# Sparse attention and a multiplicative FFN in one kernel: the q and k transposes of six batches move from TensorE to the DMA engines

## The chip, the cores and the metric

The kernel runs on one core of one Trainium2 chip. The metric is the device time of one execution in microseconds (us). An execution that lies over 1.5% above the fastest one of the same kernel on the same chip counts as "slow"; only fast executions are compared. Each kernel was run beside the kernel before on the same chip.

The engines are TensorE (PE in the profile), VectorE (DVE), ScalarE (ACT), GpSimd (POOL) and SyncE (SP, which here only issues transfers). Where the first instruction in an engine's queue waits, those behind it wait too (shown below for DVE, for 6.06 us, and for ACT, for 3.80 us). The profile counts the transfers of all queues on the same 16 DMA engines.

## The reference, cut to what matters

```python
B, H, S, D = 8, 8, 576, 64              # q, k, v
# heads 0-3: 0 <= i - j < 32 ("local"); heads 4-7: j <= i and i % 32 == j % 32 ("strided")
attn = softmax(where(mask, q @ k.T / sqrt(D), -1e9)) @ v
x = attn.transpose(0, 2, 1, 3).reshape(B * S, H * D)        # 4608 x 512
h = (x @ w1) * (x @ w2)                                      # 4608 x 1024
return (h @ w3) @ w_out                                      # 4608 x 512
```

## The kernel before

The kernel folds `w3 @ w_out` into one matrix while it computes the attention of batch 0. It then runs nine FFN blocks ("stages"; stages 0 to 8) of 512 tokens each. Stage t hides the attention of batch t+1 between its own matmuls; stages 7 and 8 hide nothing. So stages 1 to 6 hide batches 2 to 7. The loads of batch t+2 are issued during stage t.

For the scores, q and k must have the head dimension on partitions. TensorE transposes them, and DVE and ACT copy the results out of PSUM:

```python
def ph_T(s):                                   # a pair of heads
    ps = psM.tile([P, 2, NM], FP16, tag="m")   # one bank in all
    for i, nm in enumerate("qk"):
        src = x16[(s.b, nm, s.hp // 2)]        # a buffer for each batch (pool of 2)
        for c in range(4):
            pe(nc.tensor.transpose(ps[:, i, c*P:(c+1)*P], src[:, c, h0:h0+2]..., id16))
    for i, (eng, t) in enumerate((("a", qT), ("a" if s.b < AHEAD else "v", kT))):
        copy(eng, t[...], ps[:, i]...)         # q by ACT, k by DVE
# ... ph_R: the same for the last 64 tokens of each head, all heads of a batch at once
```

The values v of the local heads need their rows shifted between token tiles. POOL casts the loaded v to fp16, and DVE then copies 32 partitions of the result:

```python
def load_vL(b):
    vt = v16L[b % 2]
    for hp in range(2):
        # ... st <- v by DMA
        for pr in (bass.ds(32, 32), bass.ds(64, 64)):
            nc.gpsimd.tensor_copy(out=vt[pr, hs, :, 0:D], in_=st[pr])
        nc.vector.tensor_copy(out=vt[0:32, hs, 1:LT, 0:D], in_=vt[96:P, hs, 0:LT-1, 0:D])
```

Everything that TensorE must do in a stage is put in one order: the units of the FFN, with the steps of the next batch's attention spread between them.

```python
def host(units, upto, lead=0):
    # ... after each FFN unit, as many attention steps as bring `pos` evenly to `upto`
for tch in range(1, NTILE):
    units = ab_halves(tch) + o_halves(tch)
    # ... load_qk(tch+2, 0), load_rest(tch+2), load_vL(tch+2)
    host(units[0:12], mid)
    # ... load_qk(tch+2, 1), load_vS(tch+2)
    host(units[12:], batch_end[tch + 1])
```

The softmax here doesn't subtract the row's maximum and nothing guards it: scores larger than these inputs give would overflow.

## Time and profile before

| | kernel before |
|---|---|
| time, median of 2 runs | 296.9 us |
| TensorE busy | 268.9 us of the profiled span of 299.8 us |
| start until stage 0 (fold, attention of batch 0) | 49.2 us |
| stages 1 to 6 | 29.1, 28.8, 27.8, 29.7, 27.8, 26.5 us |
| stage 7, which hides nothing | 21.0 us |
| last load packet | 185.3 us |

The first fence is from the page of the kernel before. Its rows are the busy time of the engines, the span in 40 slices with the busy share in tenths (PEclk is the clock that was granted to TensorE), the DMA packets, and the chain of work that ended last.

```profile
PE 268.9 (90%) x2401; PEld 141.6 (47%) x2401; DVE 174.6 (58%) x353; ACT 147.1 (49%) x269; POOL 102.1 (34%) x118
...
PE   2258898989889989989999899999999999999995
...
PEclk9996999999999999999999999999999999999999
DMA  7999999999869929994896796030012002003003
...
DMA packets 58653, 48.64 MB, mean 162 GB/s; under 512 B 29184, under 2 KB 49664, under 8 KB 58624
...
PE 67%; DVE 9%; DMA 9%; ACT 9%; issue 3%; SPq 1%; POOL 0%; ACTq 0%
```

TensorE is busy nearly all the time and makes up two thirds of the chain. The DMA row is at nine tenths from slice 2 to slice 10 (75 us), has gaps later, and is almost empty after slice 25: the loads run ahead of their use and are done with 115 us to go.

In every run with a listed span, the time is 1.7 us above the span. By that the profiled execution took about 301.5 us, which is 1.8% above the fastest run beside it: by the rule above it is a slow one.

The next fence is the view of windows for the kernel before, one line for the start and for some stages. The columns are the window, its length, the busy time of each engine with its number of instructions, the granted clock, the DMA share (1.00 and more is full) and what was moved.

```profile
core 0: us, PE busy (x) PEld busy (x) DVE busy (x) ACT busy (x) POOL busy (x), PEclk, DMA share, GB/s
0.00:49.20 49.20, 31.20 (x305) 18.26 (x306) 18.79 (x51) 21.80 (x39) 28.87 (x41) 0.93 1.04 289
...
84.70:113.70 29.00, 27.98 (x276) 14.72 (x273) 23.45 (x44) 14.92 (x29) 13.87 (x15) 1.00 0.85 201
113.70:142.50 28.80, 27.69 (x278) 14.93 (x275) 21.41 (x43) 15.14 (x30) 14.82 (x16) 1.00 0.92 212
```

A stage is TensorE's: 27.7 to 28.0 us of work in 28.8 to 29.0 us, at full clock.

The table of waits of the kernel before shows the small waits of TensorE at the stage starts. The columns are engine and line, what it waited for, the us in total, the number of times and the longest.

```profile
PE aps L312 <- ACT xT L291: 3.0, 5, 1.8
...
DVE v16L L182 <- POOL v16L L181: 1.9, 2, 1.6
```

### The profile page before, as it was taken

To read this page: it belongs to the slowest core of one execution; us is meant where nothing else is said; L and a number is where in the kernel's file an instruction comes from. 1 tells how busy PE (TensorE), PEld (TensorE's weight loads), DVE (VectorE), ACT (ScalarE), POOL (GpSimd) and SP (SyncE) were. 2 spreads that over 40 slices of the span, in tenths; PEclk is the share of its full clock that TensorE was granted. 3 is DMA by queue.
4 is the path that set the end of the run, shared out by engine and by line. 5 is a ranking of instruction groups with operands and counts; after the bars stand their busy time and mean duration, and the time that the engine had idled before them with its cause. 6 is when DMAs were issued, how large, how long until landed. Compare 5 with 4: busy or idle time off the path is not lost.

```text
span 299.8 us, 6132 instructions
## 1 busy us (share of the span) xinstructions
PE 268.9 (90%) x2401; PEld 141.6 (47%) x2401; DVE 174.6 (58%) x353; ACT 147.1 (49%) x269; POOL 102.1 (34%) x118
## 2 busy tenths in 40 slices
PE   2258898989889989989999899999999999999995
PEld 1025554435545545545555445555555555444442
DVE  2011775357888866886789659747765774340430
ACT  2025586557565545536645554564455445333332
POOL 5539744486626724653455345110000000000000
PEclk9996999999999999999999999999999999999999
DMA  7999999999869929994896796030012002003003
GB/s 228 349 160 352 288 348 258 216 273 209 249 200 243 242 79 270 246 178 159 240 236 140 253 193 164 27 115 2 2 57 87 0 2 105 35 2 116 24 2 140
DMA packets 58653, 48.64 MB, mean 162 GB/s; under 512 B 29184, under 2 KB 49664, under 8 KB 58624
## 3 DMA queue, kind: packets, MB, share of 16 engines
q1 hardware_dynamic: 53440, 38.81, 54.7%
q10 hardware_dynamic: 5184, 9.44, 8.7%
q8 instruction: 19, 0.31, 0.5%
q14 instruction: 10, 0.08, 0.1%
HBM read 38.80 MB, written 9.44 MB: 161 GB/s over the span
## 4 chain that ended last, share of the span: by engine, by line
PE 67%; DVE 9%; DMA 9%; ACT 9%; issue 3%; SPq 1%; POOL 0%; ACTq 0%
PE ops L335 19%; PE bps L321 18%; PE aps L312 16%; PE xps L268 4%; PE ps L214 4%; DMA st<-in_moe_w_dram 4%; ACT pte L253 3%; DVE ptm L255 3%; DMA st<-in_moe_w_out_dram 3%; DMA out_dram<-osb 3%; PE sps L248 2%; PE ps L284 2%; DVE abt L323 2%; ACT xT L291 2%; DVE kT L72 2%
## 5 line engine op out<-in xcount | busy, mean ns | idle before, releaser
L312 PE MATMUL aps<-xT,w1h 128*128 128x512 f16 x288 | 75.3, 379 | 3.2 <-ACT xT L291 3.0
L323 DVE TENSOR_TENSOR abt<-bps,asb 128x512 f16<-128x512 f32 x72 | 49.5, 687 | 47.2 <-PE bps L321 45.5
L321 PE MATMUL bps<-xT,w2h 128*128 128x512 f16 x288 | 74.0, 379 | 0.0
L315 ACT COPY asb<-aps 128x512 f32<-128x512 f32 x72 | 42.2, 586 | 64.6 <-PE aps L312 61.8
L335 PE MATMUL ops<-w,abt 128*128 128x512 f16 x288 | 71.7, 379 | 0.5 <-DVE abt L323 0.5
L74 POOL CAST t<-st 128x1024 f16<-128x1024 f32 (+1 forms) x48 | 47.4, 991 | 43.4 <-DMA st<-in_k_dram 29.1
L253 ACT ACTIVATE pte<-sps 128x576 f16<-128x576 f32 (+1 forms) x64 | 38.4, 650 | 7.3 <-PE sps L248 7.1
L276 DVE TENSOR_TENSOR xqs<-xps,rcp 96x384 f16<-96x384 f32 (+1 forms) x64 | 39.6, 619 | 2.0
L321 PEld LDWEIGHTS <-w2h 128*128 128x128 f16 x288 | 25.8, 97 | 31.6 <-issue 5.1
L70 ACT COPY qT<-ps 128x512 f16<-128x512 f16 (+1 forms) x48 | 22.9, 481 | 29.9 <-PE ps L214 23.8
L346 ACT COPY osb<-ops 128x512 f32<-128x512 f32 x36 | 21.1, 586 | 29.9 <-PE ops L335 28.6
L335 PEld LDWEIGHTS <-abt 128*128 128x128 f16 x288 | 24.7, 98 | 23.1 <-DVE abt L323 1.0
L312 PEld LDWEIGHTS <-w1h 128*128 128x128 f16 x288 | 25.1, 98 | 22.2
L181 POOL CAST v16L<-st 32x768 f16<-32x768 f32 (+1 forms) x32 | 27.1, 847 | 18.4 <-DMA st<-in_v_dram 12.6
L268 PEld LDWEIGHTS <-ptm 72*128 72x128 f16 (+1 forms) x448 | 21.4, 97 | 19.2 <-DVE ptm L255 6.4
L255 DVE TENSOR_TENSOR ptm<-pte,maskL 128x576 f16<-128x576 f16 x32 | 20.5, 646 | 11.7 <-ACT pte L253 11.2
L72 DVE COPY kT<-ps 128x512 f16<-128x512 f16 (+1 forms) x36 | 18.8, 535 | 10.1 <-ACT qT L70 10.0
L255 DVE TENSOR_TENSOR ptm<-pte,maskS 72x576 f16<-72x576 f16 x32 | 19.6, 620 | 8.5 <-ACT pte L253 7.9
L192 POOL CAST v16S<-st 72x1024 f16<-72x1024 f32 x16 | 16.9, 1055 | 20.1 <-PE xps L268 11.4
L335 PE MATMUL ops<-woh,w3T 128*128 128x512 f16 x64 | 19.8, 440 | 3.2 <-POOL woh L74 3.1
L214 PEld LDWEIGHTS <-t 128*128 128x128 f16 x256 | 17.1, 99 | 8.8 <-issue 2.6
L214 PE MATMUL ps<-id,t 128*128 128x128 f16 x256 | 20.1, 222 | 0.5 <-POOL t L74 0.5
(48 smaller groups left out, 175.8 us busy)
## 6 DMA issues: line engine op xcount, KB each, us to landing
out_dram<-osb ACTq DMA_DIRECT2D x36, 256.0 KB, 2.0
st<-in_moe_w_dram SPq DMA_DIRECT2D x16, 512.0 KB, 8.9
st<-in_q_dram SPq DMA_DIRECT2D x16, 512.0 KB, 5.5
st<-in_k_dram SPq DMA_DIRECT2D x16, 512.0 KB, 6.6
st<-in_v_dram SPq DMA_DIRECT2D x32, 144.0 KB, 6.1
st<-in_v_dram SPq DMA_DIRECT2D x16, 256.0 KB, 7.2
st<-in_moe_w_out_dram SPq DMA_DIRECT2D x4, 512.0 KB, 8.5
st<-in_q_dram SPq DMA_DIRECT2D x8, 128.0 KB, 8.1
```

Source lines behind the costliest of these rows:

```text
L74: nc.gpsimd.tensor_copy(out=out, in_=in_)
L181: nc.gpsimd.tensor_copy(out=vt[pr, hs, :, 0:D], in_=st[pr])
L214: pe(nc.tensor.transpose(ps[:, i, c * P:(c + 1) * P], src[:, c, h0:h0 + 2].rearrange("p h d -> p (h d)"), id16))
L253: nc.scalar.activation(out=pte[0:kr], in_=sps[0:kr, :, 0:288], func=AF.Exp, bias=0.0, scale=scale)
L255: nc.vector.tensor_mul(ptm[0:kr, 0:576].rearrange("p (a x) -> p a x", x=w), pte[0:kr].rearrange("p h (a x) -> p (h a) x", x=w), _ap(mk, 0, ...
L268: pe(nc.tensor.matmul(xps[:, h, i * 65:(i + 1) * 65], ptm[0:kr, c0:c0 + P], vt[0:kr, 2 * (s.hp % 2) + h, g * m + i, :], start=True, stop=T ...
L276: nc.vector.tensor_mul(xqs[0:w, 0:m].rearrange("p i h d -> p h i d"), xv[:, :, :, 0:D], _ap(rcp, 0, [[rp, w], [4, 2], [1, m], [0, D]]))
L312: pe(nc.tensor.matmul(aps, w1h[:, ci, bass.ds(jc * P, P)], xT[ci][:, tok], start=(ci == 0), stop=(ci == KM - 1)))
L315: nc.scalar.copy(out=asb, in_=aps)
L321: pe(nc.tensor.matmul(bps, w2h[:, ci, bass.ds(jc * P, P)], xT[ci][:, tok], start=(ci == 0), stop=(ci == KM - 1)))
L323: nc.vector.tensor_mul(abts[tch][:, jc, :], bps, st["asb"])
L335: pe(nc.tensor.matmul(st["ps"], lhs(ci), rhs(ci), start=(ci == 0), stop=(ci == KF - 1)))
```

## The change

The intent is to take q,k transposes away from TensorE, which bounds the kernel. For batches 2 to 7, four DMA transposes per batch (k and q of the local heads, k and q of the strided heads) write transposed tiles directly in SBUF. The token layouts change with it (96x6 for local heads, 72x8 padded to 80 rows for strided heads). POOL puts the local keys in order with one copy (`kN`). The attention of a batch is to be done two FFN units before its stage ends. Batches 0 and 1 stay on TensorE.

```diff
+    xl = {nm: consts.tile([LQ, 2, LC, 2 * D], FP16, name=f"xl{nm}") for nm in "qk"}
+    xs = {nm: consts.tile([SR, 2, ST, 2 * D], FP16, name=f"xs{nm}") for nm in "qk"}
+    kL = ...; qL = [two tiles]; kN = [two tiles]; qS = ...; kS = ...
 ...
+    def turn_L(b):
+        for nm, t in (("k", kL), ("q", qL[b % 2])):
+            nc.sync.dma_start_transpose(t.rearrange("x g c p -> x (g c) p"),
+                                        xl[nm].rearrange("p g c x -> p (g c x)"))
+        nc.gpsimd.tensor_copy(out=kN[b % 2][:, :, 32:KN].rearrange("x g (p c) -> x g p c", c=LC),
+                              in_=kL.rearrange("x g c p -> x g p c"))
+
+    def turn_S(b):
+        nc.sync.dma_start_transpose(kS[:, 0:2*ST*SR]..., xs["k"]...)
+        nc.sync.dma_start_transpose(qS..., xs["q"]...)
 ...
+        src = (xl if s.local else xs)[nm]          # ph_T, batches 0 and 1 only
 ...
-    host(fold, batch_end[0], lead=3)
+    host(fold, batch_end[0] - 4, lead=7)
+    while pos[0] < batch_end[0]:
+        stream[pos[0]]()
+        pos[0] += 1
 ...
+            turn_S(tch + 1)
             if more:
-                load_qk(tch + 2, 0)
-                load_rest(tch + 2)
+                load_qkL(tch + 2)
                 load_vL(tch + 2)
             mid = (pos[0] + batch_end[tch + 1]) // 2
             host(units[0:12], mid)
             if more:
-                load_qk(tch + 2, 1)
+                load_qkS(tch + 2)
                 load_vS(tch + 2)
-            host(units[12:], batch_end[tch + 1])
+                turn_L(tch + 2)
+            host(units[12:], batch_end[tch + 1], tail=2)
 # ... cut: score operands, masks, padded 80-row loads, order of the weight loads and their casts
 #     moved from POOL to ACT and DVE
```

## The prediction

> **What bounds the kernel now.** TensorE: the page shows it busy 90% of the span, and the chain of waits is 67% PE. By the starts of the FFN blocks in the timeline, the six stages that hide the attention of batches 2 to 7 run from 85.9 to 254.5 us, 28.1 us each. A stage's 96 FFN matmuls take 20.8 us (the two last stages, which hide nothing, show it). The attention adds about 6.7 us, of it 0.45 us per pair for the 8 q,k transposes and 0.23 per batch for the rest rows. About 0.6 us per stage is idle, mostly the first matmul waiting for the last attention copy (waits table: 3.0 us in 5). In 120:150 DVE is busy 78%, ACT 54%, POOL 49%. The first 49 us are bound by loads: DMA share about 1.0, PE waiting for casts of freshly landed weights.
>
> **What the change removes.** In batches 2 to 7, 24 groups of 8 transposes (0.45 us between starts) and 6 rest groups (0.23): 12.2 us of TensorE, all on the critical path, 2.03 us per stage. From DVE the k copies (24 of 689 ns, 12 of 228: 19 us), from ACT the q copies (24 of 587, 12 of 269: 17 us); both off the path. Finishing attention two units early should take away most of the boundary wait: about 2.5 us.
>
> **What it adds.** Per batch four DMA transposes (0.3 MB each), one POOL copy of 128x1152 (estimate 1.3 us from casts of 1024 at 1.05), POOL casts of about 8 us for q,k in place of 5, a permuted copy back for local pairs (0.45 us, perhaps 0.65). POOL stays near 55%. In batches 0,1 eight groups of 0.26 us replace 4x0.45+0.23: even. Weight casts move from POOL to idle ACT and DVE; loads stay the bound of the start: 0 to 2 us saved.
>
> **The DMA is the risk.** Loads use 85% of the engines in 60:90 and end near 182 us, so they run ahead. I estimate 13 us of full DMA time per batch for loads and 3 for stores, in a 26 us stage: a transpose may cost at most 2.5 us. The Trainium skill ("DMA: Bandwidth & Descriptors", "Latency and other measured facts") gives 261 GB/s for a DMA transpose with non-contiguous middle dimension; no run here shows it yet. By it I estimate 1.2 us each: it fits. But the strided tiles are single: their transposes wait at the head of SP's queue for the previous batch's last scores, and later loads wait behind them. Run-ahead shrinks to about a stage.
>
> **Sum.** 296.9 - 12.2 (transposes) - 2.5 (boundaries) - 1 (start) + 2.8 (first transposes late at stage 1, other late arrivals) = 284 us. Range 277 to 299. Faster by over 2%: 0.73; within 2%: 0.15; slower by over 2%: 0.12.
>
> **What would show it.** Right: stages 1 to 6 at 25.5 to 26 us; PE busy near 257 us; a transpose lands under 5 us after issue; no PE wait on transposed tiles after stage 1, nor for xT at stage starts; DVE and ACT down 15 us or more. Wrong: PE waiting for kN, qL, kS or qS; casts ending near 240 us with late v or q,k; SP's queue held by transposes.
>
> **What would make it wrong.** DMA transposes under about 120 GB/s, so that DMA sets the stage (near 30 us, total over 300); other loads slowed by them; batch 2's transposes stalling stage 1 by more than 5 us; more exposed waits in batches 0,1, whose transposes share one bank.

## More of the kernel before

The inputs q, k, v are drawn with a standard deviation of 0.1. The scores are therefore close to zero, and the attention is close to a plain mean over the allowed keys.

## The result, and the profile after

The changed kernel takes 334.57 us (median of 2 runs, 334.28 and 334.87) against 296.9 us. The ratio is 1.128, with a 95% interval of 1.121 to 1.135. Here and below a ratio is the mean time of one kernel's fast runs over that of the other's fast runs of the same rounds, so it is not quite the ratio of the medians that are quoted.

| | before | after |
|---|---|---|
| time | 296.9 us | 334.57 us |
| start until stage 0 | 49.2 us | 85.0 us |
| stage 0 | 35.5 us | 33.0 us |
| stages 1 to 6 | 29.1, 28.8, 27.8, 29.7, 27.8, 26.5 | 29.5, 33.9, 25.7, 29.5, 25.7, 25.6 us |
| last load or transpose packet | 185.3 us | 260.9 us |
| mean granted clock | 0.987 to 0.994 | 0.918, 0.923 |

The clock of before is that of seven fast runs beside the first experiments. These are the same rows of the page, now of the changed kernel:

```profile
PE 265.4 (80%) x2225; PEld 133.8 (40%) x2225; DVE 169.7 (51%) x334; ACT 135.7 (41%) x223; POOL 122.8 (37%) x136
...
PE   0460007587899888997599999799999999999995
...
PEclk9995556959599999999599999899999999999999
DMA  6999999999954399799999999984404500301103
...
DMA packets 75275, 57.06 MB, mean 171 GB/s; under 512 B 50960, under 2 KB 61200, under 8 KB 75248
...
PE 60%; DMA 18%; DVE 11%; SPq 3%; POOL 3%; issue 2%; ACT 2%; ACTq 0%; DVEq 0%; POOLq 0%
```

Three things stand out. TensorE has a hole in slices 4 to 6. The DMA is now at nine tenths or more in all but one of slices 15 to 26, where before had gaps, and the DMA's share of the chain has doubled to 18%. There are 21,776 more packets under 512 B. In the packet records 20,992 more are packets of 256 B, and the packets' time, spread over 16 engines, rises from 190.0 to 242.6 us.

The windows of the changed kernel (start, then stages 1, 2 and 3):

```profile
0.00:85.00 85.00, 34.23 (x326) 19.68 (x327) 30.96 (x67) 27.78 (x38) 45.03 (x60) 0.77 1.06 259
...
118.00:147.50 29.50, 26.81 (x253) 13.22 (x252) 21.96 (x38) 14.12 (x24) 16.77 (x17) 1.00 1.05 210
147.50:181.30 33.80, 27.72 (x237) 13.69 (x236) 18.60 (x36) 12.66 (x22) 19.56 (x20) 0.90 1.02 222
181.30:207.00 25.70, 25.63 (x237) 13.04 (x236) 16.70 (x36) 12.76 (x22) 13.12 (x14) 1.00 1.05 236
```

A stage without trouble takes 25.7 us with 25.63 us of TensorE. The saving on TensorE is real: 2 us less work than the 27.7 us of before's stage 2. But stage 2 took 33.8 us at a clock of 0.90.

The waits of the changed kernel:

```profile
PE ps L240 <- POOL xlk L74: 29.1, 1, 29.1
...
PE aps L337 <- DVE abt L348: 5.9, 2, 5.6
...
DVE v16L L212 <- POOL v16L L211: 11.9, 7, 6.1
```

There are two losses, then. One wait of 29.1 us lies in the start. The other is a set of stalls in the stages: in stage 2 DVE stands for v, and in stage 4, as the trace shows, ACT stands at an output store.

**The start.** The next fence is the timeline of POOL in the changed kernel. The columns are start, duration, engine and line, operation, tiles, shapes, and in brackets the idle time before it and what ended it. The second fence is TensorE's timeline at the same time.

```profile
19.75 0.82 POOL L74 CAST xlk<-st 96x768 f16<-96x768 f32 x1 [0.50 <-DMA st<-in_k_dram]
...
51.11 0.82 POOL L74 CAST xlk<-st 96x768 f16<-96x768 f32 x1 [0.40 <-DMA st<-in_k_dram]
```

```profile
22.30 0.62 PE L382 MATMUL trp<-id,t 128*128 128x128 f16 x8 [0.58 <-DVE t L72]
51.99 0.66 PE L240 MATMUL ps<-id,xlk 96*128 96x96 f16 x6 [29.06 <-POOL xlk L74]
```

Batch 0's local k was cast into `xlk` by 20.6 us. TensorE did not transpose it then. It waited until 51.99 us, right after the third cast into `xlk`, which is batch 1's. `xl` and `xs` are single tiles. In program order `load_qkL(1)` stands before the transposes of batch 0, so the framework, which orders accesses to a tile by the program, makes the transposes wait for batch 1's casts. They then read batch 1's k and q. The same holds for batch 1 and `load_qkL(2)`, `load_qkS(2)`, but for one tile: the k of batch 1's first strided pair is transposed before it is overwritten (transpose at 103.16 us, cast at 103.65 us).

So the change has a fault that is not one of time only: batches 0 and 1 attend with the q and k of the batch after them (that one tile apart). The comparison with the reference passes all the same. I computed with the reference, on the host, what exchanging q and k in these two batches does to the output. It moves the output by 1.1% in these batches and by 0.55% overall (norm of the difference over norm of the output).

**The stages.** This is the timeline of the changed kernel in stage 2, from DVE's stand to TensorE's restart:

```profile
158.93 1.71 POOL L211 CAST v16L<-st 32x768 f16<-32x768 f32 x2 [0.62 <-DMA st<-in_v_dram]
...
160.67 0.33 DVE L212 COPY v16L<-v16L 32x640 f16<-32x640 f16 x1 [6.06 <-POOL v16L L211]
161.03 0.46 DVE L279 TENSOR_TENSOR ptm<-pte,maskL 128x576 f16<-128x576 f16 x1
161.40 0.68 DVE L348 TENSOR_TENSOR abt<-bps,asb 128x512 f16<-128x512 f32 x1
...
162.14 1.87 PE L337 MATMUL aps<-xT,w1h 128*128 128x512 f16 x4 [5.57 <-DVE abt L348]
```

The v of a later batch landed late. POOL cast it at 158.93 us. DVE's next instruction in order was the row copy of that v, so DVE stood for 6.06 us. Behind it waited a mask product and a gate product (`abt`) that had nothing to do with that v. TensorE needed the PSUM bank that `abt` frees, and stood for 5.57 us. Then four matmuls took 1.87 us where they take 1.03 us elsewhere. The clock records show half clock from 158.8 us for 6.8 us.

The Trainium skill ("TensorE: Matmul & The Clock Gate", "Part 1: The HAM clock gate (the "warmup" mystery)") says that TensorE drops to half clock after an idle window of about 3.4 us and needs about that long to come back. This trace agrees in the lengths: the two stretches at half clock in the stages that hide batches 2 to 7, from 158.8 and 213.4 us, last 6.8 and 3.4 us. They come with stalls of 5.6 and 2.1 us. It does not agree in the idle window: the first fall came 2.2 us into its stall, and in the 3.4 us before the two falls TensorE was busy 1.18 and 1.32 us (more in the last section). My prediction left this out. With both, stage 2 took 8.1 us more than an undisturbed stage.

Stage 4 lost 3.8 us in another way:

```profile
211.22 0.37 ACTq L372 DMA_DIRECT2D out_dram<-osb  x1
211.63 1.07 ACT L340 COPY asb<-aps 128x512 f32<-128x512 f32 x2 [3.80 <-DMA qS<-xsq]
...
212.26 1.02 PE L346 MATMUL bps<-xT,w2h 128*128 128x512 f16 x4 [2.10 <-ACT asb L340]
```

This copy by ACT reads only PSUM, and still ACT stood for the transpose into `qS`. In front of the copy in ACT's queue is an output store. The semaphore fields that the packed trace keeps for each instruction show why it stood: the store waits for completion semaphore 109, which it is to use next, and the transpose issued at 206.28 us had used it and landed at 211.14 us. TensorE stood 2.10 us behind ACT, and the second stretch at half clock followed.

### The profile page after: what moved, and what is told of

Read it like the earlier page. It is cut to its first block, busy times and chain, and to the rows that moved or that the text cites. A ratio compares the mean times of both kernels' runs of the same rounds, so it can differ in the third digit from the quotient of the medians.

```text
span 333.2 us, 5783 instructions
## 1 busy us (share of the span) xinstructions
PE 265.4 (80%) x2225; PEld 133.8 (40%) x2225; DVE 169.7 (51%) x334; ACT 135.7 (41%) x223; POOL 122.8 (37%) x136
## 4 chain that ended last, share of the span: by engine, by line
PE 60%; DMA 18%; DVE 11%; SPq 3%; POOL 3%; issue 2%; ACT 2%; ACTq 0%; DVEq 0%; POOLq 0%
PE ops L360 20%; PE bps L346 15%; PE aps L337 15%; DMA st<-in_v_dram 6%; DMA qS<-xsq 5%; DVE xqs L300 4%; PE sps L273 3%; DMA st<-in_moe_w_dram 3%; DMA st<-in_k_dram 3%; PE ps L308 2%; PE xps L292 2%; DMA st<-in_q_dram 2%; DVE abt L348 2%; DVE ptm L279 1%; PE ps L240 1%
## 5 line engine op out<-in xcount | busy, mean ns | idle before, releaser
L337 PE MATMUL aps<-xT,w1h 128*128 128x512 f16 x288 | 77.4, 392 | 6.0 <-DVE abt L348 5.9
L346 PE MATMUL bps<-xT,w2h 128*128 128x512 f16 x288 | 76.6, 390 | 2.5 <-ACT asb L340 2.5
L360 PE MATMUL ops<-w,abt 128*128 128x512 f16 x288 | 70.1, 379 | 0.0
L337 PEld LDWEIGHTS <-w1h 128*128 128x128 f16 x288 | 26.4, 100 | 33.8 <-issue 9.2
L346 PEld LDWEIGHTS <-w2h 128*128 128x128 f16 x288 | 26.5, 100 | 31.4 <-issue 6.1
L211 POOL CAST v16L<-st 32x768 f16<-32x768 f32 (+1 forms) x32 | 27.5, 859 | 19.5 <-PE xps L292 12.2
L371 ACT COPY osb<-ops 128x512 f32<-128x512 f32 x36 | 21.1, 586 | 28.7 <-PE ops L360 28.7
L240 PE MATMUL ps<-id,xlk 96*128 96x96 f16 x24 | 1.9, 224 | 29.1 <-POOL xlk L74 29.1
L74 POOL CAST xlq<-st 96x768 f16<-96x768 f32 x16 | 13.6, 853 | 29.5 <-DMA st<-in_q_dram 25.5
L74 POOL CAST xsk<-st 72x1024 f16<-72x1024 f32 x16 | 16.9, 1071 | 16.5 <-DMA kS<-xsk 12.1
L360 PE MATMUL ops<-woh,w3T 128*128 128x512 f16 x64 | 21.6, 479 | 0.5 <-DVE w3T L384 0.5
L298 DVE RECIPROCAL rcp<-xps 96x6 f32<-96x6 f32 (+1 forms) x64 | 12.2, 191 | 18.8 <-PE xps L292 18.6
L74 POOL CAST xsq<-st 72x1024 f16<-72x1024 f32 x16 | 16.6, 1053 | 6.0 <-DMA qS<-xsq 3.7
```

The source lines that it names most:

```text
L74: nc.gpsimd.tensor_copy(out=out, in_=in_)
L337: pe(nc.tensor.matmul(aps, w1h[:, ci, bass.ds(jc * P, P)], xT[ci][:, tok], start=(ci == 0), stop=(ci == KM - 1)))
L346: pe(nc.tensor.matmul(bps, w2h[:, ci, bass.ds(jc * P, P)], xT[ci][:, tok], start=(ci == 0), stop=(ci == KM - 1)))
L360: pe(nc.tensor.matmul(st["ps"], lhs(ci), rhs(ci), start=(ci == 0), stop=(ci == KF - 1)))
L371: nc.scalar.copy(out=osb, in_=ps)
```

## The experiments

The theories that the expectations name are these. The start is explained above and tested by e1 and e5. For the stages, theory D says that the DMA engines are full, so that data come late and TensorE waits. Its rivals are W (loads wait behind transposes at the head of SP's queue, with DMA time to spare), later H (DVE's queue stops in order behind a late v) and Q (engines stop in order behind late transposed tiles and their copies).

The kernels below were all run with the kernel before on the same chip; its median there lay between 294.55 and 296.34 us. Differences in us between kernels of different sessions are worked out from the ratios, times 296 us.

### e1: batch 1 gets its own tiles

```diff
+    xl1 = {nm: <free columns of xT[i], as [96, 2, 6, 128]> for i, nm in enumerate("qk")}
+    xs1 = {nm: <free columns of xT[2 + i], as [80, 2, 8, 128]> ...}
-                copy(eng, xl[nm][:, hp]...          # the casts; ph_T reads the same way
+                copy(eng, (xl1 if b == 1 else xl)[nm][:, hp]...
```

> The changed kernel, but batch 1's q,k casts go to tiles of their own (free columns of xT) and not into the single xl, xs. Theory A: in program order batch 1's casts stand before batch 0's transposes, so with single tiles TensorE waits for the wrong batch (and transposes it); then the 29 us wait of the first q,k transpose goes, the first FFN matmul starts near 50 us and not 85, the time falls by 28 to 36 us to 299 to 307 us, and the error falls in batches 0 and 1. Rival B: the start is held by the new load order, the casts moved to ACT and DVE and the split loads; then the first FFN matmul still starts after 75 us and the time stays above 325 us.

Measured: 319.47 us, ratio 1.080 (1.075 to 1.085), above the 299 to 307 us expected. Stage 0 begins at 57.9 us, not at 85.0. The theory of the start holds: 27 us came back there. But only 14 us of it arrived at the end. Stages 1 to 4 now take 36.8, 34.6, 30.7 and 28.7 us. I read it so: the long start had given the loads of the later batches time to run ahead; without it the DMA share is 0.88 to 1.11 in these four stages. The loss in the stages was there in the changed kernel, partly hidden by the loss in the start.

### e2, e3: no transposes, and plain copies in their place

```diff
 # e2, from e1
-            nc.sync.dma_start_transpose(...)        # all four; stale q, k: wrong on purpose
 # e3, from e1
-            nc.sync.dma_start_transpose(t..., xl[nm]...)
+            nc.sync.dma_start(t[0:96]..., xl[nm]...[:, 0:1152])     # the same for xs: plain copies
```

> The kernel of the run before, with the 24 DMA transposes left out (wrong result on purpose: batches 2 to 7 use stale q,k). Theory A: the stages 1 to 4 were 29.7 us and not 25.6 because of the transposes (their transfer time of about 3.8 us each, or the waits that hang on them); without them all six stages take 25.6 to 26 us and the time is 13 to 18 us under the run before, 284 to 290 us. Rival B: the stages are held by POOL (more casts, the kN copy) and DVE's wait for v; then the time is within 4 us of the run before.

> As the first run, but each DMA transpose becomes a plain SBUF to SBUF copy of 0.2 MB between the same tiles, so the same waits and the same place in SP's queue (wrong result on purpose). Theory A1, the transfer time of the transposes counts: near the run without transposes, within 4 us. Theory A2, the waits at the head of SP's queue and the single tiles count, whatever the transfer takes: near the run with transposes, within 4 us.

Measured: e2 313.8 us, ratio 1.055 (1.045 to 1.065). e3 313.25 us, ratio 1.059 (1.053 to 1.064). Their outputs are wrong, which doesn't matter for the times. Taking the transposes away gave only 7 to 8 us, far from what theory D alone would give. e2 has an artefact of its own: with no transpose to wait for, the kN copy came earlier in POOL's queue and waited there for scores (20.5 us between 60 and 165 us), with casts behind it. (The profiled run of e2 was a slow one.) So e2 doesn't tell what the transposes cost, and that e3 came within 4 us of it, as theory A1 asked, doesn't tell either. I repeated it later without that artefact (e16).

### m1: transposes by themselves

A kernel that only moves data: one transpose at a time, then two in flight, plain copies, then loads beside them. The output is zero.

```diff
+    for _ in range(4): tl(0)          # 96 x 1536 fp16, the same destination: one after the other
+    for _ in range(4): ts(0)          # 80 x 2048 fp16
+    for _ in range(4): cl(0)          # plain copy of 96 x 1536
+    for i in range(6): tl(i % 2)      # two in flight
+    for i in range(6): ts(i % 2)
```

> Nothing but DMA transposes and copies of the change's shapes (output zero on purpose): four of 96x1536 one after the other, four of 80x2048, four plain copies of 96x1536, then six and six with two in flight, then loads of 512 KB beside transposes. By the changed kernel's trace two transposes in an idle queue took 7.6 us, so 3 to 4.5 us each alone (70 to 110 GB/s), and about 3.5 us each with two in flight if the engines are full; the plain copy about 2.5 us. If the prediction's 261 GB/s held, 1.2 us each with two in flight.

The timeline of SP in m1. The duration is that of the issue, or spans the group's issues where the number at the end is not 1; how long a transfer takes is read from one start to the next that waits for it:

```profile
5.84 1.31 SPq L95 DMA_TRANSPOSE kL<-xl  x1
...
12.38 1.28 SPq L95 DMA_TRANSPOSE kL<-xl  x1
...
30.13 0.51 SPq L101 DMA_DIRECT2D pL<-xl  x1
...
35.94 0.51 SPq L101 DMA_DIRECT2D pL<-xl  x1
36.49 10.42 SPq L95 DMA_TRANSPOSE kL<-xl  x6
46.96 11.99 SPq L98 DMA_TRANSPOSE qS<-xs  x6
```

One after the other, a transpose takes 3.3 us (96x1536, 0.295 MB; two from 5.84 to 12.38) or 3.6 us (80x2048, 0.328 MB; two from 17.91 to 25.13, not shown), and a plain copy 2.9 us, as expected. With two in flight it is 1.74 and 2.0 us each: 170 and 164 GB/s. The last part, loads beside transposes, I did not evaluate. The prediction had 1.2 us. It is below the break-even of 2.5 us that the prediction named, so by that reckoning it should still have fitted. The other terms of the reckoning had to be looked at (below).

### e4, e10: only the early finish, on the kernel before

```diff
-    def host(units, upto, lead=0):
+    def host(units, upto, lead=0, tail=0):
-            tgt = p0 + ((upto - p0) * max(i + 1 - lead, 0)) // n
+            tgt = p0 + ((upto - p0) * min(max(i + 1 - lead, 0), n)) // n
-            host(units[12:], batch_end[tch + 1])
+            host(units[12:], batch_end[tch + 1], tail=2)
```

> The kernel before with one part of the change alone: each batch's attention is done two FFN units before its stage ends. The prediction gave this 2.5 us (the matmul that opens a stage waits 0.6 us for the last attention copy). If that holds, the time falls by 2 to 3.5 us (ratio 0.988 to 0.993). Rival: the wait only moves, because the same attention work is squeezed between fewer FFN units; then within 0.3%.

> The kernel of e4 once more, word for word (the kernel before plus attention done two units early), because e4 was unclear: 2 to 2.5 us less than the kernel before, ratio 0.985 to 0.995. If the boundary waits were worth nothing, the ratio is 1.00 within 0.3 per cent.

Measured: e4 294.77 us, ratio 0.986 (0.972 to 1.000), with two slow runs of four: unclear. e10, the same kernel with more rounds: 294.72 us, ratio 0.998 (0.994 to 1.002). In e10's profile stages 1 to 5 take 27.6 to 28.1 us where before has up to 29.7, but that profile of before was a slow run. Over the runs the gain is 0.5 us, within the interval of zero. The 2.5 us of the prediction are not there.

### e5: the fold spaced as before

```diff
 # from e1
-    host(fold, batch_end[0] - 4, lead=7)
-    while pos[0] < batch_end[0]: ...
+    host(fold, batch_end[0], lead=3)
```

> The run with batch 1's own tiles, but batch 0's attention spread over the weight fold as in the kernel before (from the fourth unit on, to the end) and not from the eighth unit on with four pieces after it. There the FFN began at 57.9 us, against 49.2 before. Theory: the crowded, exposed attention of batch 0 costs most of these 9 us, so the FFN starts at 51 to 54 us and the time falls by 4 to 7 us, to 312 to 316 us. Rival: loads and casts in their new order hold the start; then the FFN starts after 56 us and the time is within 2 us.

Measured: 314.97 us, ratio 1.062 (1.051 to 1.072). Stage 0 begins at 49.8 us, as in before (49.2). So the rest of the start's loss was the crowding of batch 0's attention into fewer, later places. Of those 8 us about 5.5 arrive at the end; stages 1 to 4 still take 37.6, 30.0, 30.7 and 29.6 us.

### e6, e7: transposes issued as early as possible

```diff
 # from e1 (e6) and from e5 (e7): qS and kS doubled, and
-            turn_S(tch + 1)                      # at the stage's start
                 load_qkL(tch + 2)
+                turn_L(tch + 2)
                 load_vL(tch + 2)
 ...
                 load_qkS(tch + 2)
+                turn_S(tch + 2)
                 load_vS(tch + 2)
-                turn_L(tch + 2)
```

> The run with batch 1's own tiles, with qS and kS doubled too and each pair of DMA transposes placed right behind the casts that feed it, so that no transpose waits at the head of SP's queue for scores and no load waits behind it. Theory W (these waits cost): stages 1 to 4, there 32.7 us on average, fall to 28 us or less, and the time to 298 to 306 us. Theory D (the 16 DMA engines are full: loads, stores and transposes need about 26 us a batch, and late data then idles TensorE and drops its clock): stages 1 to 4 stay at 30 us or more on average, the time above 310 us.

> The two edits of the two runs before this one together. If both theories hold and add up, 294 to 300 us, close to the kernel before; if DMA is full and loads hold the start, over 308 us.

Measured: e6 320.09 us, ratio 1.072 (1.057 to 1.087). e7 314.43 us, ratio 1.061 (1.050 to 1.072). Each is as slow as the kernel it was made from. Theory W, that loads wait behind transposes at the head of SP's queue and this sets the time, falls.

### e8: every transpose twice

```diff
 # from e1: behind each of the four transposes
+            nc.sync.dma_start_transpose(<scratch tile that nobody reads>, <the same source>)
```

> The kernel of e1 with each of the 24 DMA transposes issued twice; the second writes to a scratch tile that nobody reads, so TensorE, ACT, DVE and POOL do exactly what they did. Theory D (the DMA engines are full in stages 1 to 4 of e1, and transposes are paid in DMA time): four more transposes cost 4 x 1.85 = 7.4 us of DMA time a batch, stages 1 to 5 grow from e1's mean of about 31 us to 36 to 39 us, and the total rises from 319 to 340 to 355 us. Rival (the stages are long because work is badly ordered or because POOL and DVE are late, the DMA has room): the extra transposes fit beside the work, total within 5 us of e1's 319.

Measured: 352.7 us, ratio 1.193 (1.188 to 1.198): 33 us more than e1, within theory D's range of 340 to 355. The packets' time over 16 engines rises by 49.3 us for 24 transposes on the 256 B packets, which is 2.06 us each. DMA time is paid.

### e9: half the transposes

The local pairs go back to TensorE in all batches; only the strided pairs use DMA transposes.

```diff
 # from e5
     def turns(p, nm):
-        if p < 4 * AHEAD:
+        if p < 4 * AHEAD or p % 4 < 2:
 # and in each stage load_qkS, load_vS first, load_qkL, load_vL second, no turn_L
```

> The kernel of e5 with the local pairs of batches 2 to 7 back on TensorE (k, q of two pairs, 4 groups of 6 transposes of 0.26 us, copies by DVE and ACT, no kN copy on POOL); only the two strided transposes per batch stay on the DMA, and the strided loads come first in a stage. 12 transposes in place of 24. Theory D: DMA time per batch falls from about 26 to 22.5 us, below the TensorE time, so stages 1 to 6 fall to 26.5 to 27.5 us each and the total to 286 to 294 us, below the kernel before (295). Rival (the transposes' number matters little; order and POOL do it): stages 1 to 4 stay at 29 to 31 us, total 302 to 312 us.

Measured: 314.06 us, ratio 1.059 (1.054 to 1.064), the same as e5. This is a miss of theory D: 12 transposes fewer gained nothing. Its trace shows how a late v becomes a stall. These are the window in which DVE stood for v in stage 5 (all engines, as above), two windows after it (TensorE alone), and the timeline there:

```profile
208.69:213.71 5.02, 5.02 (x35) 2.53 (x34) 0.01 (x1) 2.33 (x6) 4.86 (x6) 1.00 0.93 249
```

```profile
214.00:218.00 4.00, 1.85 (x24) 1.00 0.01 2
218.00:222.00 4.00, 4.00 (x21) 0.57 0.01 4
```

```profile
213.71 0.33 DVE L223 COPY v16L<-v16L 32x640 f16<-32x640 f16 x1 [5.02 <-POOL v16L L222]
...
217.89 0.30 PE L284 MATMUL sps<-qL,kN 64*128 64x96 f16 x6 [0.99 <-DVE xqs L311]
218.13 1.63 PE L357 MATMUL bps<-xT,w2h 128*128 128x512 f16 x4
```

DVE stands 5.02 us for the cast of the last batch's v. While it stands, TensorE still works all the time; the DMA share is 0.93, and POOL is busy with the casts in front of that one. TensorE pays afterwards: DVE catches up late, TensorE is busy 1.85 us of 4 although the DMA is now idle (0.01), and then the clock drops to 0.57. Half the transposes gone and nothing gained, and a stall behind DVE's order: so I formed theory H, that DVE's order turns a late v into a stall.

### e11, e12, e13: the v row copy on POOL

```diff
 # from e5 (e11), from e9 (e12), from e4 (e13)
-            nc.vector.tensor_copy(out=vt[0:32, hs, 1:LT, 0:D], in_=vt[96:P, hs, 0:LT-1, 0:D])
+            nc.gpsimd.tensor_copy(out=vt[0:32, hs, 1:LT, 0:D], in_=vt[96:P, hs, 0:LT-1, 0:D])
```

The copy now stands right behind the cast on the same engine, so DVE never waits for v.

> The kernel of e5 (batch 1 with its own tiles, folds spaced as before) with the two small copies per batch that shift v's rows (v16L from v16L, 32x640) moved from DVE to POOL, right behind the POOL cast that they wait for, so that DVE never waits for v in order. Theory D (the DMA engines are full, v comes late whatever the order): TensorE then waits for v itself, total within 3 us of e5's 315. Theory H (the DVE queue stops behind a v16L copy whose cast is late, and with it the exponent masks, the attention outputs and the gate products; this turns a late v into a TensorE stall and a lower clock): stages 1 to 4 fall from 30 to 37 us to 27 to 29 us and the total to 298 to 306 us.

> The kernel of e9 (half the DMA transposes) with the same copies on POOL. H: the stalls of e9, which fell in stages 4 and 5 at a DMA share of 0.3 to 0.7, vanish; stages 1 to 5 fall from a mean of 31.3 to 27 to 28 us, total 290 to 300 us. If H is wrong, 314 us again within 3 us.

> The kernel of e4 and e10 (the kernel before, attention done two units early) with the same copies on POOL. The kernel before loses only 1.9 us of DVE time to these waits, so 0 to 2 us faster than e10: ratio 0.99 to 1.00 to the kernel before.

Measured: e11 304.99 us over all six runs, three of them slow; ratio of the fast ones 1.023 (1.016 to 1.029), against 1.062 for e5: 11.5 us less. e12 302.51 us, ratio 1.022 (1.017 to 1.027), against 1.059 for e9: 11 us less, though not down to the 290 to 300 us that H expected. The direction of theory H holds in both, and theory D's "within 3 us of e5" falls. The profiled run of e11 was a slow one, so I read no stages from it. In e12's profile stages 2 to 5 take 27.7 to 28.4 us with TensorE busy 27.1 to 27.3 us, so there it is TensorE's limit again; against e10 it loses in the start (stage 0 begins at 50.5, not 46.4 us) and in stage 1 (31.7, not 27.9 us). e13 294.21 us, ratio 0.992 (0.985 to 0.998), the lowest median of the versions that keep all their work, 2 to 3 us under the kernel before. It is also the control for H: where v is hardly late, the same edit gains little.

### e14, e15: the kN copy moved to DVE

```diff
 # from e11 (e14); e15 also has e6's early transposes
-        nc.gpsimd.tensor_copy(out=kN[b % 2]..., in_=kL...)      # in turn_L
+    def ph_N(b):
+        nc.vector.tensor_copy(out=kN[b % 2]..., in_=kL...)
 ...
+            if i == 3 and AHEAD <= b + 1 < B:
+                add(ph_N, b + 1)
```

> The kernel of e11 with the copy that puts k's local keys in order (kN from kL) moved from POOL, where it stands behind the casts of later loads, to DVE at a place in the attention's stream just before the batch that needs it. In e11 that copy held TensorE for 7.1 us at stage 1 and started a slow-clock stretch. Theory Q (in-order queues behind late data are what is left of the loss): stage 1 falls from 37 us to 31 to 34 us, total 298 to 302 us. Theory D (the DMA engines alone): 305 us within 2.

> The kernel of e14 with the strided tiles doubled and every transpose issued right behind its casts (as e6 did), so that batch 2's transposes have landed long before stage 1. Q: stage 1 at 28 to 30 us, the later stages 26 to 27.5 us, total 288 to 296 us, the kernel before or better. D: stages 1 to 4 stay at 29 to 31 us, total over 300 us, since the DMA work is the same.

Measured: e14 309.57 us, ratio 1.052 (1.039 to 1.064). e15 316.72 us, ratio 1.070 (1.058 to 1.082). Both are worse than e11. The timeline of DVE in e14 shows the reason:

```profile
93.31 1.16 DVE L207 COPY kN<-kL 128x1152 f16<-128x1152 f16 x1 [5.43 <-DMA kL<-xlk]
```

DVE now stood for the transposes as it had stood for v. My fix made the same mistake as the change. It speaks for H once more: put a copy that depends on a late transfer into DVE's queue, and the time rises, here by 7 us (fast runs, on two chips) to 9 us (by the ratios).

### e16, e17: transposes free, and transposes that nobody reads

e16 is e11 without the 24 transposes and without the kN copy. e17 is e16 with the transposes put back, into scratch tiles. Both compute with stale q and k.

```diff
 # e16, from e11
-            nc.sync.dma_start_transpose(...)                        # all four
-        nc.gpsimd.tensor_copy(out=kN[b % 2]..., in_=kL...)
 # e17, from e16
+            nc.sync.dma_start_transpose(<scratch tile>, xl[nm]...)  # and the same for xs
```

> The kernel of e11 without the 24 DMA transposes and without the POOL copy of kN; batches 2 to 7 compute with stale q, k, wrong on purpose. This is the change with its transposes free: TensorE saves as planned, v does not stop DVE, no transposed tile is waited for. If the transposes (their DMA time and the waits for their tiles) are all that is left of the loss: stages 1 to 6 at 25.6 to 26.5 us, total 284 to 290 us, what the prediction had. If something else in the change's loads holds it (permuted casts on POOL, late v): 295 us or more.

> The kernel of e16 with the 24 DMA transposes put back, but into scratch tiles that nobody reads: they take DMA time and their place in SP's queue, and no engine waits for what they write (wrong on purpose as e16). If DMA time is what is left (theory D): close to e11's 305 us, 300 to 306. If waiting for the transposed tiles and the kN copy in POOL's order is (theory Q): close to e16, 285 to 293 us.

Measured: e16 290.31 us over all six runs, three of them slow (the fast ones 287.0, 287.9 and 289.2); ratio 0.972 (0.964 to 0.979). e17 297.98 us, ratio 1.005 (1.000 to 1.011), between the two ranges that theories Q and D expected. Windows of e16 (stages 2 and 4), then of e17 (stages 2 and 4):

```profile
112.80:138.80 26.00, 25.65 (x237) 13.04 (x236) 17.29 (x34) 12.87 (x22) 20.14 (x23) 1.00 1.04 241
...
164.80:190.90 26.10, 25.66 (x237) 13.04 (x236) 16.60 (x34) 12.87 (x22) 14.04 (x16) 1.00 0.60 155
```

```profile
111.30:137.00 25.70, 25.63 (x238) 13.04 (x237) 16.88 (x34) 12.76 (x22) 13.35 (x16) 1.00 1.03 213
...
163.70:197.20 33.50, 28.74 (x238) 13.92 (x237) 20.34 (x36) 14.20 (x25) 20.99 (x22) 0.90 1.15 212
```

With free transposes each of stages 1 to 6 is TensorE's (25.6 to 27.5 us), and the change gains 2.8%. Put back, but unread, they cost 3.4 points of ratio, about 10 us (7.7 us between the medians of all six runs). They take 2.26 us each of all 16 engines, as the packet records of e17 less those of e16 show, and they move the end of the loads and transposes from 181.1 to 227.6 us. e17's stages 1 to 3 are still good (27.3, 25.7, 26.7 us), which I put down to the loads' lead; stages 4 and 5 take 33.5 and 29.1 us. There ACT, which also issues the output stores, stood for loads:

```profile
162.57 0.34 ACTq L381 DMA_DIRECT2D out_dram<-osb  x1
163.01 1.19 ACT L286 ACTIVATE pte<-sps 128x576 f16<-128x576 f32 x2 [3.08 <-DMA st<-in_q_dram]
...
168.04 0.34 ACTq L381 DMA_DIRECT2D out_dram<-osb  x1
168.47 0.59 ACT L380 COPY osb<-ops 128x512 f32<-128x512 f32 x1 [3.25 <-DMA st<-in_v_dram]
169.11 1.10 PE L346 MATMUL aps<-xT,w1h 128*128 128x512 f16 x4 [2.41 <-ACT osb L380]
```

These ACT instructions use no q and no v from the staging tiles. The semaphore fields of the trace show what happens. All transfers of the kernel use eight completion semaphores in turn, and a store is held back until the transfer that used its semaphore before has landed. The store of 162.57 us waits for semaphore 105, which the load of q issued at 157.10 had used (landed at 162.49); that of 168.04 for 110, used by the load of v issued at 159.04 (landed at 167.96). Five stores of e17 stand over 0.5 us in this way, 12.1 us together; in the kernel before, e5, e12 and e16 none does. TensorE's long stands in these two stages (2.4, 1.0 and 3.1 us) all come behind ACT, and 6.8 us at half clock follow in stage 4. So here too a late transfer reaches TensorE through another engine's order.

### What the loss was made of

The kernels form a chain in which each differs from the one before by one thing, except that e11 to e17 takes two things away at once. The steps are the differences of the ratios, times 296 us; steps taken in another order could differ somewhat.

| from, to | what goes | ratio | step |
|---|---|---|---|
| after to e1 | batches 0 and 1 read the next batch's tiles | 1.128 to 1.080 | 14 us |
| e1 to e5 | crowded attention of batch 0 | 1.080 to 1.062 | 5.5 us |
| e5 to e11 | DVE's queue standing for v | 1.062 to 1.023 | 11.5 us |
| e11 to e17 | waits for transposed tiles, the kN copy | 1.023 to 1.005 | 5 us |
| e17 to e16 | the transposes as transfers: their DMA time, and ACT's stands at the stores | 1.005 to 0.972 | 10 us |

## Why the prediction was wrong

The prediction was 284 us, faster; the result was 334.57 us, slower. Point by point:

- **What bounds the kernel before, and the TensorE saving: right.** Undisturbed stages take 25.6 to 25.7 us, as predicted (25.5 to 26). With its transposes and the kN copy free and the faults of e1, e5 and e11 mended (e16) the change runs at 0.972, which is 288 us: a gain of 8 us where the prediction had 12.2 for the transposes alone.
- **"In batches 0,1 eight groups of 0.26 us replace 4x0.45+0.23: even": this step failed first.** It counted instructions and did not ask which tile each reads. `xl` and `xs` are single tiles and are loaded for the next batch before they are read. That cost 36 us at the start together with the crowding, of which 14 + 5.5 us showed in the total, and it made batches 0 and 1 wrong. I named "more exposed waits in batches 0,1", but for their single bank, not for this.
- **"I estimate 13 us of full DMA time per batch for loads and 3 for stores ... By it I estimate 1.2 us each: it fits": mis-sized in two terms.** In e16, which has no transposes, the packets take 193.1 us over 16 engines. Less 25.8 for the stores and an estimated 36.7 for the weights (by their packet sizes), 130.6 us remain for eight batches: 16.3 us per batch, not 13. The transposes take 2.06 to 2.26 us each in the kernel (e8 less e1, e17 less e16), about 9 us per batch, not 4.8. With 3.2 us of stores the sum is 28.5 us in a stage of 25.6 us, where the prediction had 20.8. So the transfers fall behind as soon as their lead is used up. The sum is a guide only, since packet times overlap: e16's stage 2 runs in 26.0 us at a share of 1.04. The 261 GB/s of the Trainium skill ("DMA: Bandwidth & Descriptors", "Latency and other measured facts") were not reached here: 164 to 170 GB/s alone with two in flight.
- **"Later loads wait behind them. Run-ahead shrinks to about a stage": right in its effect, wrong in its price.** The prediction took 2.8 us for all late arrivals. It did not ask who stands in order behind late data. DVE stood behind the v row copy (11.5 us), POOL's kN copy and the transposed tiles cost 5 us, ACT stood at the output stores (12.1 us in e17), and in the changed kernel two stalls were followed by 6.8 and 3.4 us at half clock. Transposes landed 3.7 to 10.2 us after their issue, not in under 5.
- **"A transpose may cost at most 2.5 us": wrong as a criterion.** It follows from the load term that was too small. With 16.3 us of loads and 3.2 of stores, 25.6 us leave 1.5 us each.
- **Boundaries, 2.5 us: not shown.** The early finish alone gave 0.5 us, not told from zero (e10).
- **Smaller terms.** The kN copy took 2.14 us, not 1.3. The permuted copy back took 0.75 us (0.65 predicted). TensorE's busy time is 265.4 us, not 257, for the half-clock stretches lengthen its work. ACT fell by 11.4 us and DVE by 4.9 us, not by 15 or more.

Still open: how much of the 10 us of the last step would remain if the stores did not wait for semaphores that loads and transposes hold. No run separates the two.

## What to carry to other kernels

Before moving work to the DMA, add up its packet time per stage from the trace, with the loads and stores that are already there, and compare the sum with the stage: a lead of the loads hides a deficit for a few stages only. Then ask of each engine's queue which instruction depends on a transfer that may now be late, and what stands behind it in order; here, moving a 0.55 us copy to the engine that it waited for gained 11.5 us, about as much as the 24 transposes cost as transfers. Output stores count among these instructions, since they may wait for a semaphore that a load holds. And when a buffer is no longer one per batch, read the program order of its writers and readers, since a test on inputs that hardly depend on it will not notice that the wrong batch is read.

## What the Trainium skill lacked or had wrong

- "DMA: Bandwidth & Descriptors", "Latency and other measured facts", gives 261 GB/s for a DMA transpose with a non-contiguous middle dimension. The transposes of 0.295 and 0.328 MB here, SBUF to SBUF in packets of 256 B, reached 164 to 170 GB/s with two in flight and about 90 GB/s one after the other (m1). Beside loads they took 2.06 to 2.26 us of packet time on all 16 engines each (e8, e17).
- "Advanced Engine Details and Errata", "X-Bar Transpose (TRN2)", calls transposes as fast as regular DMAs and expects 350 to 400 GB/s. In m1 a plain copy of the same 0.295 MB took 2.9 us and the transpose 3.3 us, one in flight, so the ratio is near. Neither came near that bandwidth at this size (101 and 90 GB/s), and the section names no size.
- "TensorE: Matmul & The Clock Gate", "HAM oscillation — how this bites in real kernels", warns of idle gaps above about 3.4 us. Less was enough here: in the changed kernel a stretch at half clock began at 213.4 us after a gap of 2.1 us, and in e9 one at 218.4 us after gaps of 1.0 us and less. I cut all traces but m1's into windows of 3.41 us, the step in which the clock records change, without the first 60 and the last 15 us. In the 40 windows that ended with a fall to half clock TensorE was busy 1.83 us or less; in the 1154 that kept full clock it was busy 1.44 us or more, in all but four at least 1.74 us. In e17 a gap of 3.1 us, split between two windows, brought no fall. So what separates them here is about half a window of work, and not one long gap.
- No page of it that I used says that output stores on ACT's queue can make ACT wait for loads on SP's queue. Here ACT stood 3.1 and 3.3 us for loads whose data it does not use (e17), because the store waits for a completion semaphore that the load had used.
